# Scores in groups of three key chunks, and PSUM as three shared two-bank tiles: attention followed by an MLP mixer on one core

## The chip, the cores and the metric

The kernel runs on one core of one Trainium2 chip. The metric is the device time of one execution in microseconds (us), the median of several. The granted TensorE clock of one and the same kernel (its mean over the span, as a share of full speed) differs a little from run to run, mostly between 0.98 and 1.00, and so does the time.

Engine names in the profile: PE is TensorE's matmuls, PEld its weight loads, DVE is VectorE, ACT is ScalarE, POOL is GpSimd, SP the engine that issues most DMAs. Tile names: psS are scores, psO attention products, psR and psU the two token products (`tok1`, `tok2`), psG and psF the two channel products (`m_ch1`, `m_ch2`), pst and psT transposes. DVE evicts psO into x, psR into rt and psU into u; qk is the transposed q and k of a pair, pt the Exp of scores, gt the ReLU of psG, ost an output tile.

## The reference

Batch 8, 12 heads, 448 positions, head size 64; then a mixer MLP with 256 token units and 1536 channel units over the model width of 768.

```python
q_n = q / (norm(q) + 1e-6);  k_n = k / (norm(k) + 1e-6)
attn = softmax(q_n @ k_n.T / tau)
x    = concat_heads(attn @ v)                    # (8, 448, 768)
h    = relu(x.T @ w_tok1) @ w_tok2               # over positions
u    = x + h.T
out  = u + relu(u @ w_ch1) @ w_ch2               # over channels
```

## The kernel before

Work goes by pairs of heads, 48 of them (6 for each batch). The instructions of each engine are issued in the order in which the program writes them. For a pair there are four *score chunks* (112 keys by 448 queries, for two heads), each evicted by one Exp, then two *attention products* (`pv`, one for each head), two *token products* (`tok1`, `tok2`). The channel MLP of an earlier batch is cut into *units*, and units are fed in between, so that TensorE has something to do while other engines evict.

PSUM has eight banks. The Trainium skill, "PSUM — Partial Sum Buffer", section "Specifications (TRN2)", gives the same: 8 banks in a partition, 512 FP32 values each; the tiles of either kernel fill just eight. Before the change they are four single banks (`ps`, for everything but scores) and two two-bank tiles (`ps2`, for scores only).

```python
ps  = ctx.enter_context(tc.tile_pool(name="ps",  bufs=4, space=bass.MemoryType.PSUM))
ps2 = ctx.enter_context(tc.tile_pool(name="ps2", bufs=2, space=bass.MemoryType.PSUM))
# [cut]
def score(i, c):
    qk = pipe[i]["qk"][:].rearrange("p a c s -> p (a c s)")
    psS = ps2.tile([128, 2, 512], FP32, name=f"psS_{i}_{c}", tag="s")
    for hh in range(2):
        hb = hh * 64
        nc.tensor.matmul(psS[:, hh, 0:S], qk[hb:hb + 64, c * SC:c * SC + 128],
                         qk[hb:hb + 64, S:2 * S], start=True, stop=True)
    nc.scalar.activation(out=pts[i % 2][...], in_=psS[0:SC, :, 0:S], func=AF.Exp, scale=inv_tau)
# [cut: pv -> psO -> x by DVE; tok1 -> psR -> rt by DVE; tok2 -> psU -> u by DVE]
def m_ch1(b, ct):                                   # one unit: one bank
    psG = ps.tile([128, S], FP32, name=f"psG_{b}_{ct}", tag="b")
    for dt in range(DT):                            # 6 matmuls of 448 columns
        nc.tensor.matmul(psG[:], wc1t[...], ut[b][...], start=(dt == 0), stop=(dt == DT - 1))
    nc.scalar.activation(out=gt[...], in_=psG[:], func=AF.Relu)

def m_ch2(b, m, dh):                                # one unit: one bank
    psF = ps.tile([128, DH], FP32, name=f"psF_{b}_{m}_{dh}", tag="b")
    for ct in range(CT):                            # 12 matmuls of 384 columns
        nc.tensor.matmul(psF[:], gt[:, ct, lo:lo + 128], wc2t[...], start=(ct == 0), stop=(ct == CT - 1))
    # [cut: DVE adds u; for m == 3 in two adds of 64 partitions; after dh == 1 the DMAs out]
# [cut]
# main loop, pairs 7 to 48 (side work on q, k, v cut)
    score(i, 0); score(i, 1)
    feed(quota * 0.22)
    pv(i - 1, 0); pv(i - 1, 1)
    feed(quota * 0.28, least)
    score(i, 2); score(i, 3)
    feed(quota * 0.25, least)
    tok1(i - 1)
    feed(quota * 0.25, least)
    tok2(i - 1)
```

## Time and profile before

| | before |
|---|---|
| time, median of 3 first runs | 408.08 us (407.75 to 409.68) |
| span of the profiled run | 406.0 us, clock 0.982 |
| PE busy | 389.1 us, 96% |
| ACT, POOL, DVE busy | 59%, 54%, 51% |

These lines are from the page of the kernel before: the busy time of PE with its share of the span and its count of instructions, then the span in 40 slices, with the busy tenths of PE and the granted clock in tenths.

```profile
PE 389.1 (96%) x4146; PEld 240.4 (59%) x4146; DVE 206.4 (51%) x441; ACT 240.8 (59%) x392; POOL 218.5 (54%) x257
...
PE   6978799999999999999999999999999999999995
...
PEclk9868999999999999999999999999999999999999
```

PE is at 9 (90% or more) from slice 6 to the last but one. The clock is down only in the slices between 10 and 40 us; the trace has it halved from 9.1 to 12.5 and from 22.7 to 33.0 us.

The table by stretches of the same kernel: the stretch in us from the start, its length, then the busy time (and count) of PE, PEld, DVE, ACT and POOL, then the clock and the DMA share and rate.

```profile
62.00:100.00 38.00, 36.60 (x437) 22.84 (x435) 23.44 (x46) 27.54 (x55) 29.84 (x33) 1.00 0.98 208
100.00:140.00 40.00, 40.00 (x435) 23.79 (x432) 20.21 (x45) 27.44 (x44) 23.49 (x27) 1.00 0.79 165
...
300.00:340.00 40.00, 40.00 (x425) 24.18 (x425) 18.34 (x46) 22.11 (x33) 15.53 (x19) 1.00 0.47 102
```

In the stretches of 40 us shown PE is busy all the time. A busy PE is not by itself a PE at its peak, because the ends of matmuls are modelled. So the starts were read from the trace too. From one matmul to the next they are at the streaming rate: psG (448 columns) 189 ns, psF (384) 162, psR and psU (128) 56, psO (65) 29 to 33. Around scores they are not: the last matmul before a score takes 95 ns more than its rate, and the last score before another product takes 93 ns more.

The groups of instructions that matter, from the page: line, engine, operation, tiles, shapes, count, then busy us, mean ns of one, and after the second bar the idle time before them with its main releaser.

```profile
L321 PE MATMUL psG<-ut,wc1t 128*128 128x448 f16 x576 | 122.4, 353 | 0.0
L336 PE MATMUL psF<-wc2t,gt 128*128 128x384 f16 x672 | 116.6, 326 | 0.0
...
L340 DVE TENSOR_TENSOR ost<-psF,u 128x384 f32<-128x384 f32 (+1 forms) x64 | 35.7, 557 | 96.2 <-PE psF L336 96.0
L324 ACT ACTIVATE gt<-psG 128x448 f16<-128x448 f32 x96 | 52.3, 545 | 53.7 <-PE psG L321 53.5
...
L256 PE MATMUL psS<-qk 64*128 64x448 f16 x384 | 56.2, 363 | 3.5 <-ACT pt L258 2.7
```

PE has 3.5 us of idle time before scores in the whole span. Three lines of PE's timeline in the steady part (start, length, line, operation, count):

```profile
195.44 0.55 PE L256 MATMUL psS<-qk 64*128 64x448 f16 x4
195.92 1.19 PE L272 MATMUL psO<-vt,pt 112*128 112x65 f16 x32
196.95 1.30 PE L321 MATMUL psG<-ut,wc1t 128*128 128x448 f16 x6
```

A group of four score matmuls (two chunks) starts at 195.44 and the next product at 195.92. Two heads' matmuls run side by side in two halves of the array's rows, so two chunks take two streams of 0.19 us, which is 0.38; the group takes 0.48, and the product ahead of it is stretched by 0.1 as well.

**The ledger.** From the starts as the trace has them, the time from the first MLP matmul to the last matmul can be split. For each matmul the streaming time of its own columns (two side-by-side score matmuls count as one) is subtracted from the gap to the next start; each change between scores and other products is charged 0.0945 us; what is left of a gap counts as a wait where it is over 0.03 us, else as remainder. For the kernel before:

```
                streaming   changes         waits   remainder   first MLP matmul to last matmul
before          327.75      162 = 15.31      1.81     3.69        348.56 us
```

There is next to nothing to gain but the 15.31 us of changes (the text also calls them drains). That is what the change is after.

### The profile page before, as it was taken

How to read it: one execution, taken by the hardware profiler on the slowest of the kernel's cores; microseconds unless marked ns; L12 is line 12 of the kernel's file. 1: busy time of each engine (PE TensorE's matmuls, PEld its weight loads, DVE VectorE, ACT ScalarE, POOL GpSimd, SP SyncE). 2: the span in 40 equal slices, each digit the busy share in tenths (PEclk: the TensorE clock that was granted, in tenths of full speed). 3: DMA queues.
4: the chain of work that ended last, by engine and by line, in shares of the span. 5: the costliest groups of instructions: out<-in, count | busy, mean ns of one | idle time of the engine just before them, and what ended most of it. 6: DMA issues, size and time to landing. Idle time of an engine off the chain costs nothing.

```text
span 406.0 us, 10118 instructions
## 1 busy us (share of the span) xinstructions
PE 389.1 (96%) x4146; PEld 240.4 (59%) x4146; DVE 206.4 (51%) x441; ACT 240.8 (59%) x392; POOL 218.5 (54%) x257
## 2 busy tenths in 40 slices
PE   6978799999999999999999999999999999999995
PEld 5656566566555665656656655556655666655562
DVE  5767877655454466554555555635636345312031
ACT  5857789954676438773587437773588535521400
POOL 7797999948557480949175852949092800000000
PEclk9868999999999999999999999999999999999999
DMA  8999999978859786867759697978974433103022
GB/s 198 239 175 251 246 262 230 209 195 180 201 142 191 140 200 157 197 161 171 201 127 187 156 184 188 164 152 187 195 130 94 114 81 92 28 15 116 2 74 81
DMA packets 102590, 64.07 MB, mean 158 GB/s; under 512 B 61328, under 2 KB 98960, under 8 KB 102544
## 3 DMA queue, kind: packets, MB, share of 16 engines
q1 hardware_dynamic: 96928, 58.22, 64.0%
q0 software_dynamic: 5616, 5.21, 8.1%
q8 instruction: 32, 0.52, 0.6%
q14 instruction: 14, 0.11, 0.1%
HBM read 43.45 MB, written 11.01 MB: 134 GB/s over the span
## 4 chain that ended last, share of the span: by engine, by line
PE 87%; DMA 5%; DVE 4%; POOL 1%; issue 1%; ACT 1%; SPq 0%; DVEq 0%; POOLq 0%
PE psF L336 27%; PE psG L321 27%; PE psO L272 12%; PE psS L256 10%; PE psU L299 5%; PE psR L285 5%; DMA kf<-in_k_dram 4%; DVE ssq L198 2%; DMA qf<-in_q_dram 1%; DVE x L276 1%; PE pst L235 1%; POOL kq L221 0%; ACT sq L185 0%; DVE ost L340 0%; DVE rt L288 0%
## 5 line engine op out<-in xcount | busy, mean ns | idle before, releaser
L258 ACT ACTIVATE pt<-psS 112x896 f16<-112x896 f32 x192 | 166.2, 914 | 84.4 <-PE psS L256 84.1
L321 PE MATMUL psG<-ut,wc1t 128*128 128x448 f16 x576 | 122.4, 353 | 0.0
L336 PE MATMUL psF<-wc2t,gt 128*128 128x384 f16 x672 | 116.6, 326 | 0.0
L221 POOL TENSOR_TENSOR kq<-kf,rn 112x512 f16<-112x512 f32 x47 | 50.0, 1063 | 99.3 <-ACT rn L213 86.3
L336 PEld LDWEIGHTS <-gt 128*128 128x128 f16 x672 | 63.1, 98 | 43.4 <-issue 5.2
L340 DVE TENSOR_TENSOR ost<-psF,u 128x384 f32<-128x384 f32 (+1 forms) x64 | 35.7, 557 | 96.2 <-PE psF L336 96.0
L324 ACT ACTIVATE gt<-psG 128x448 f16<-128x448 f32 x96 | 52.3, 545 | 53.7 <-PE psG L321 53.5
L321 PEld LDWEIGHTS <-wc1t 128*128 128x128 f16 x576 | 51.3, 98 | 46.6 <-issue 8.2
L198 DVE TENSOR_REDUCE ssq<-sq 112x16 f32<-112x1024 f32 (+1 forms) x49 | 58.1, 1189 | 9.0 <-ACT sq L185 6.4
L272 PEld LDWEIGHTS <-pt 112*128 112x128 f16 x1536 | 53.5, 99 | 15.5 <-ACT gt L324 7.0
L256 PE MATMUL psS<-qk 64*128 64x448 f16 x384 | 56.2, 363 | 3.5 <-ACT pt L258 2.7
L272 PE MATMUL psO<-vt,pt 112*128 112x65 f16 x1536 | 59.3, 195 | 0.1
L302 DVE TENSOR_TENSOR u<-psU,x 128x512 f16<-128x512 f32 x48 | 33.1, 689 | 34.2 <-PE psU L299 34.2
L187 POOL TENSOR_TENSOR sq<-kf 112x512 f32<-112x512 f32 x46 | 47.7, 1037 | 3.9 <-DMA kf<-in_k_dram 3.4
L221 POOL TENSOR_TENSOR kq<-qf,rn 112x512 f16<-112x512 f32 x45 | 46.8, 1041 | 0.0
L288 DVE TENSOR_SCALAR rt<-psR 128x256 f16<-128x256 f32 x48 | 20.2, 421 | 46.8 <-PE psR L285 46.6
L276 DVE TENSOR_TENSOR x<-psO,rec 128x256 f16<-128x256 f32 x96 | 40.8, 425 | 3.3
L187 POOL TENSOR_TENSOR sq<-qf 112x512 f32<-112x512 f32 x39 | 40.5, 1037 | 0.0
L285 PE MATMUL psR<-x,w1t 128*128 128x128 f16 x384 | 29.8, 221 | 2.6 <-DVE x L276 2.6
L285 PEld LDWEIGHTS <-w1t 128*128 128x128 f16 x384 | 25.0, 99 | 11.6 <-issue 3.3
L299 PEld LDWEIGHTS <-w2t 128*128 128x128 f16 x384 | 25.9, 100 | 9.0 <-issue 2.1
L299 PE MATMUL psU<-rt,w2t 128*128 128x128 f16 x384 | 30.1, 223 | 0.4 <-DVE rt L288 0.2
(40 smaller groups left out, 156.0 us busy)
## 6 DMA issues: line engine op xcount, KB each, us to landing
qf<-in_q_dram SPq DMA_DIRECT2D x48, 224.0 KB, 3.8
kf<-in_k_dram SPq DMA_DIRECT2D x48, 224.0 KB, 3.7
vf<-in_v_dram SPq DMA_DIRECT2D x48, 224.0 KB, 3.7
out_dram<-ost SPq DMA_DIRECT2D x8, 336.0 KB, 3.1
wc1t<-in_moe_w_ch_dram POOLq DMA_DIRECT2D x4, 576.0 KB, 8.2
wc2t<-in_moe_w_ch_dram POOLq DMA_DIRECT2D x2, 1152.0 KB, 16.3
out_dram<-ost SPq DMA_DIRECT2D x8, 288.0 KB, 2.9
out_dram<-ost SPq DMA_DIRECT2D x8, 240.0 KB, 2.8
```

The costliest lines, as they stand in the source:

```text
L187: nc.gpsimd.tensor_mul(out=pipe[i]["sq"][:, a], in0=src, in1=src)
L198: nc.vector.tensor_reduce(out=half[i // HP]["ssq"][:, a0:a1, lo:lo + 2 * NCH], in_=pipe[i]["sq"][:, a0:a1], axis=AXX.X, op=ALU.add)
L221: (eng or nc.gpsimd).tensor_tensor(out=st["kqn"][:, a].rearrange("p c g e -> p g c e"), in0=side(i, a), in1=_bcast_free(rn, E), op=ALU.mult)
L256: nc.tensor.matmul(psS[:, hh, 0:S], qk[hb:hb + 64, c * SC:c * SC + 128], qk[hb:hb + 64, S:2 * S], start=True, stop=True)
L258: nc.scalar.activation(out=pts[i % 2][:, 2 * S * c:2 * S * (c + 1)].rearrange("p (h s) -> p h s", h=2), in_=psS[0:SC, :, 0:S], func=AF.Exp ...
L272: nc.tensor.matmul(psO[:, m, 0:E + 1], pts[i % 2][:, at:at + 128], vt[:, g, c, 0:E + 1], start=(c == 0), stop=(c == NCH - 1))
L276: nc.vector.tensor_tensor(out=st["x"][:, :, hh * E:(hh + 1) * E], in0=psO[:, :, 0:E], in1=_bcast_free(rec[:], E), op=ALU.mult)
L285: nc.tensor.matmul(psR[:, tt], w1t[:, w1[m], tt * 128:(tt + 1) * 128], st["x"][:, m], start=(m == 0), stop=(m == 3))
L299: nc.tensor.matmul(psU[:, m], w2t[:, tt, lo:lo + 128], st["rt"][:, tt], start=(tt == 0), stop=(tt == TT - 1))
L321: nc.tensor.matmul(psG[:], wc1t[:, dt, ct * 128:(ct + 1) * 128], ut[b][:, dt].rearrange("p m s -> p (m s)")[:, lo:lo + S], start=(dt == 0) ...
L324: nc.scalar.activation(out=gt[:, ct, (b % 2) * S:(b % 2 + 1) * S], in_=psG[:], func=AF.Relu)
L336: nc.tensor.matmul(psF[:], gt[:, ct, lo:lo + 128], wc2t[:, ct, dh * DH:(dh + 1) * DH], start=(ct == 0), stop=(ct == CT - 1))
```

## The change

Scores go in groups of three chunks, across the borders of pairs, so that there are fewer changes between scores and the rest. Three chunks need three two-bank tiles, which leaves two single banks. The MLP units are therefore made twice as large (two banks each) and share the three big tiles; a fixed pattern is replaced by a loop that goes by groups. The core of the diff, cut:

```diff
-    ps = ...tile_pool(name="ps", bufs=4, ...PSUM)
-    ps2 = ...tile_pool(name="ps2", bufs=2, ...PSUM)
+    ps = ...tile_pool(name="ps", bufs=2, ...PSUM)
+    ps2 = ...tile_pool(name="ps2", bufs=3, ...PSUM)
@@ [cut: three pt buffers; warm-up matmuls allot a tile each, 8 more of them in each of pairs 2 to 5, 10 fewer ahead of the loop] @@
     def m_ch1(b, ct):
-        psG = ps.tile([128, S], FP32, name=f"psG_{b}_{ct}", tag="b")
+        psG = ps2.tile([128, 2, 512], FP32, name=f"psG_{b}_{ct}", tag="s")
+        for j in range(2):
             [6 matmuls into bank j]
-        nc.scalar.activation(out=gt[:, ct, ...], in_=psG[:], func=AF.Relu)
+        nc.scalar.activation(out=gt[:, ct:ct + 2, ...], in_=psG[:, :, 0:S], func=AF.Relu)
@@ [cut: m_ch2 likewise, psF of two banks, one DVE add of 768 columns; m == 3: two adds of 64 partitions, for two batches] @@
+    def feed():                       # once a group, at least one unit
+        fed[0] += fed[1]
+        done = 0
+        while queue and (done == 0 or fed[0] > queue[0][0] / 2):
+            t, fn = queue.pop(0)
+            fn()
+            fed[0] -= t
+            done += 1
+
+    def refill(b):                    # at tok2 of a batch's last pair
+        while queue:
+            queue.pop(0)[1]()
+        queue.extend((ch2_units(b - 1) if b else []) + ch1_units(b))
+        fed[:] = [0.0, sum(t for t, _ in queue) / 8]
+        if b == B - 2:
+            queue.extend(ch2_units(b))
@@ main loop @@
+        chunks = [(i, c) for i in range(NPAIR + 1, NP_ALL) for c in range(NCH)]
+        groups = [chunks[j:j + 3] for j in range(0, len(chunks), 3)]
+        while u_next < NP_ALL:
+            [score() of the group; side work]
+            r_ok, u_ok = p_next, r_next
+            if seen.get(p_next, g) < g:          # all four chunks in earlier groups
+                pv(p_next, 0); pv(p_next, 1); p_next += 1; r_ok = p_next
+            elif r_next < p_next:
+                tok1(r_next); r_next += 1; u_ok = r_next
+            elif u_next < r_next:
+                tok2_of(u_next); u_next += 1
+            feed()
+            while u_next < u_ok: tok2_of(u_next); u_next += 1
+            while r_next < r_ok: tok1(r_next); r_next += 1
+            g += 1
```

## The prediction

> **What bounds the kernel now.** TensorE. The table by stretches shows PE busy 40.0 of 40 us in nearly every stretch from 100 to 340 us, at clock 1.00; ACT is busy 59%, DVE 51%. Idle PE lies before 62 us (about 10 us) and in the last 4 us. Starts of consecutive matmuls in the trace are at the streaming rate (psG 189 ns, psF 162, psO 32, psU and psR 56) except around scores: the last matmul before a score takes 95 ns more, the last score 93 ns more (282 instead of 189). The Trainium skill, "TensorEngine Tiling (Array Packing)", Key Properties, says that a change of tiling mode drains TensorE; scores are 64-row tiles, all else is not. The trace agrees: 0.189 us per score group, on the critical engine.
>
> **Removed.** Pairs 7 to 47 have 82 groups of two chunks now, 55 groups after: 27 x 0.189 = 5.1 us, all on the critical path. Fewer, wider evictions (a 448-wide ReLU takes 545 ns, an 896-wide Exp 914) save ACT and DVE: no gain.
>
> **Added, by mistake.** The refill for batch 6 puts batch 6's second channel product at the end of the queue; the refill for batch 7 empties the queue and puts the same product in again. Three units run twice: 72 matmuls of 162.5 ns = 11.7 us of PE, where PE has no idle time. The result stays right.
>
> **Added waits.** A group of three needs all three two-bank tiles, and the third is the one that the latest MLP unit filled. From that unit's last matmul start the trace has 0.38 us to the eviction; with 0.92 us for a wide ReLU (0.96 for a wide add, estimates) and 0.05 back, the tile is free 1.17 us after the unit's end. PE covers 0.475 us with two chunks and the drain, and 0.45 by each token product between. In program order the steady cycle is four groups for three pairs:
> - two groups end in both token products: no wait;
> - one ends in one: 0.24 us;
> - one has no attention product and nothing behind its unit: 0.69 us before the next third chunk, and 0.31 us before its own unit, which meets the first Exp still running.
> 1.24 us per cycle, 12 cycles: 15 us. Adds in two 64-partition halves (twice 0.96 us) and DVE lateness with two small PSUM banks instead of four: 5.5 us. Groups 6 to 8 find the queue empty and wait for Exp: 1.5 us. Together 22 us.
>
> **Start.** Three score tiles remove waits for Exp of 0.6 to 0.8 us, but two small banks tie PE to DVE, and warm-up matmuls are added (1.8 us, partly in idle time). Net 0, give or take 4. The half clock at 23 to 33 us may move.
>
> **Sum.** 408.1 - 5.1 + 11.7 + 22 = 436.7 us. Prediction 437, range 424 to 449. Faster by over 2%: 1%; within 2%: 4%; slower by over 2%: 95%.
>
> **What would show it.** 744 psF matmuls instead of 672; idle time before score matmuls rising from 3.5 us to over 10, released by ReLU (gt), output add (ost) or Exp (pt); PE busy near 92% instead of 96%, with dents between 60 and 340 us; the drain still near 93 ns per edge, but a third rarer; the end, after the last token product, about 12 us longer.
>
> **What would make it wrong.** If waits hide behind each other or wide evictions free their tile sooner, only the repeat less the drains remains (about 415). If two banks make PE wait for DVE at every attention product, it exceeds 450. If the queue repeats nothing, it is about 425.

## The result

| | before | after |
|---|---|---|
| time, median (lowest to highest), 4 runs each | 408.86 us (407.75 to 409.68) | 436.80 us (436.64 to 439.99) |
| ratio of the means, 95% interval | | 1.070 (1.065 to 1.076), slower |
| span of the profiled run, clock | 406.0 us, 0.982 | 434.9 us, 0.999 |
| PE busy | 389.1 us, 96% | 401.6 us, 92% |

A ratio is always the mean time of one kernel's fast runs over that of the other's of the same rounds, so it is not quite the ratio of the medians that are quoted.

The same lines of the page after the change:

```profile
PE 401.6 (92%) x4240; PEld 253.0 (58%) x4240; DVE 203.9 (47%) x412; ACT 234.8 (54%) x344; POOL 218.4 (50%) x258
...
PE   7787899789999998999999989999999989999995
...
PEclk9999999999999999999999999999999999999999
```

PE has dents now, an 8 in the busy tenths at almost regular distances, and 94 more instructions. By stretches:

```profile
62.00:100.00 38.00, 33.74 (x429) 21.77 (x428) 23.58 (x50) 29.12 (x53) 30.74 (x34) 1.00 0.92 194
...
140.00:180.00 40.00, 37.30 (x400) 23.36 (x397) 18.36 (x37) 19.53 (x26) 22.97 (x26) 1.00 0.74 178
...
300.00:340.00 40.00, 38.69 (x416) 24.00 (x415) 17.65 (x37) 25.09 (x35) 20.52 (x24) 1.00 0.46 104
...
380.00:420.00 40.00, 40.00 (x236) 22.95 (x235) 7.53 (x8) 5.50 (x6) 0.00 (x0) 1.00 0.20 60
```

Each stretch of 40 us between 100 and 380 us has lost one to three microseconds of PE; the one after 380 us is full. The groups:

```profile
L333 PE MATMUL psF<-wc2t,gt 128*128 128x384 f16 x744 | 124.7, 326 | 0.4 <-ACT pt L257 0.2
L321 PE MATMUL psG<-ut,wc1t 128*128 128x448 f16 x576 | 114.5, 352 | 0.2
...
L324 ACT ACTIVATE gt<-psG 128x896 f16<-128x896 f32 x48 | 44.0, 916 | 79.0 <-PE psG L321 78.5
L337 DVE TENSOR_TENSOR ost<-psF,u 128x768 f32<-128x768 f32 (+1 forms) x35 | 33.5, 957 | 113.1 <-PE psF L333 113.0
...
L255 PE MATMUL psS<-qk 64*128 64x448 f16 x384 | 55.0, 357 | 11.3 <-DVE ost L337 4.8
```

There are 744 psF matmuls where there were 672: 72 more, three units of 24. The idle time before scores is 11.3 us where it was 3.5, and its main releaser is the output add. The view of waits, PE's only (who waited for what, total us, how many times, longest):

```profile
PE psS L255 <- DVE ost L337: 4.8, 8, 0.7
PE psS L255 <- ACT gt L324: 4.2, 6, 1.6
PE pst L235 <- DVE rt L287: 3.7, 4, 1.1
PE psU L298 <- DVE rt L287: 3.0, 5, 0.7
```

And the timeline of the stretch after one of the units with half-partition adds:

```profile
161.48 1.94 DVE L337 TENSOR_TENSOR ost<-psF,u 64x768 f32<-64x768 f32 x2 [2.64 <-PE psF L333]
...
161.73 0.61 PE L284 MATMUL psR<-x,w1t 128*128 128x128 f16 x8
...
162.27 0.55 PE L255 MATMUL psS<-qk 64*128 64x448 f16 x4
...
163.48 0.36 PE L255 MATMUL psS<-qk 64*128 64x448 f16 x2 [0.66 <-DVE ost L337]
...
164.53 0.61 PE L298 MATMUL psU<-rt,w2t 128*128 128x128 f16 x8 [0.69 <-DVE rt L287]
...
164.97 2.43 PE L321 MATMUL psG<-ut,wc1t 128*128 128x448 f16 x12
...
167.44 0.92 ACT L324 ACTIVATE gt<-psG 128x896 f16<-128x896 f32 x1 [2.24 <-PE psG L321]
...
168.41 0.36 PE L255 MATMUL psS<-qk 64*128 64x448 f16 x2 [0.52 <-ACT gt L324]
```

Four score matmuls (two chunks) start at 162.27 and run at once. The third chunk starts at 163.48 and not at 162.65, because its tile is the one that the psF unit filled and DVE's two adds (from 161.48, 1.94 us) have not left it yet. `rt` comes behind them on DVE, and psU waits for it. After the psG unit of 164.97, with no product between it and the next group, the third chunk waits again, for the ReLU of 167.44 (0.92 us).

The idle time in these views is smaller than the wait. The view says 0.66 us before the chunk at 163.48, while its start is 0.82 us late. Matmuls' ends are modelled later than the next one could start: one of 448 columns is shown as 0.36 us and streams 0.19. The Trainium skill, "Perfetto Trace Analysis", section "Per-instruction lifecycle: what the profiler-reported window actually captures", says that TensorE's end time is estimated; this trace agrees. The ledger, which goes by starts, is used for sizes below:

```
                streaming   changes         waits   remainder   first MLP matmul to last matmul
before          327.75      162 = 15.31      1.81     3.69        348.56 us
after           339.26      108 = 10.21     25.21     3.23        377.90 us
difference      +11.51            -5.10    +23.40    -0.46        +29.34 us
```

Ahead of the first MLP matmul the changed kernel is 0.5 us earlier (50.0 against 50.5 us from the first warm-up matmul), so the spans differ by 28.9 us.

### The profile page after: what moved, and what is told of

The parts are those of the page before. It is cut to its first block, busy times and chain, and to the rows that moved or that the text cites. A ratio compares the mean times of both kernels' runs of the same rounds, so it can differ in the third digit from the quotient of the medians.

```text
span 434.9 us, 10171 instructions
## 1 busy us (share of the span) xinstructions
PE 401.6 (92%) x4240; PEld 253.0 (58%) x4240; DVE 203.9 (47%) x412; ACT 234.8 (54%) x344; POOL 218.4 (50%) x258
## 4 chain that ended last, share of the span: by engine, by line
PE 44%; POOL 20%; issue 19%; DVE 8%; DMA 5%; ACT 3%; SPq 0%; POOLq 0%; DVEq 0%
PE psF L333 18%; PE psG L321 14%; POOL sq L187 9%; POOL kq L221 8%; PE psO L271 6%; DMA kf<-in_k_dram 3%; DVE ost L337 3%; PE psS L255 3%; POOL vt L176 3%; PE psU L298 2%; DVE ssq L198 2%; DMA qk<-kq 1%; DVE u L301 1%; ACT gt L324 1%; PE pst L235 1%
## 5 line engine op out<-in xcount | busy, mean ns | idle before, releaser
L257 ACT ACTIVATE pt<-psS 112x896 f16<-112x896 f32 x192 | 163.1, 917 | 95.5 <-PE psS L255 95.3
L333 PE MATMUL psF<-wc2t,gt 128*128 128x384 f16 x744 | 124.7, 326 | 0.4 <-ACT pt L257 0.2
L321 PE MATMUL psG<-ut,wc1t 128*128 128x448 f16 x576 | 114.5, 352 | 0.2
L333 PEld LDWEIGHTS <-gt 128*128 128x128 f16 x744 | 71.7, 98 | 46.7 <-issue 1.1
L324 ACT ACTIVATE gt<-psG 128x896 f16<-128x896 f32 x48 | 44.0, 916 | 79.0 <-PE psG L321 78.5
L337 DVE TENSOR_TENSOR ost<-psF,u 128x768 f32<-128x768 f32 (+1 forms) x35 | 33.5, 957 | 113.1 <-PE psF L333 113.0
L321 PEld LDWEIGHTS <-wc1t 128*128 128x128 f16 x576 | 54.5, 98 | 47.4 <-issue 0.7
L255 PE MATMUL psS<-qk 64*128 64x448 f16 x384 | 55.0, 357 | 11.3 <-DVE ost L337 4.8
L271 PEld LDWEIGHTS <-pt 112*128 112x128 f16 x1536 | 52.2, 98 | 15.5 <-issue 6.2
L255 PEld LDWEIGHTS <-qk 64*128 64x128 f16 x384 | 15.9, 94 | 35.1 <-issue 18.1
L298 PEld LDWEIGHTS <-w2t 128*128 128x128 f16 x384 | 24.3, 98 | 13.8 <-issue 8.3
```

The lines of the kernel that those rows point to most:

```text
L257: nc.scalar.activation(out=pts[i % 3][:, 2 * S * c:2 * S * (c + 1)].rearrange("p (h s) -> p h s", h=2), in_=psS[0:SC, :, 0:S], func=AF.Exp ...
L271: nc.tensor.matmul(psO[:, m, 0:E + 1], pts[i % 3][:, at:at + 128], vt[:, g, c, 0:E + 1], start=(c == 0), stop=(c == NCH - 1))
L298: nc.tensor.matmul(psU[:, m], w2t[:, tt, lo:lo + 128], st["rt"][:, tt], start=(tt == 0), stop=(tt == TT - 1))
L321: nc.tensor.matmul(psG[:, j, 0:S], wc1t[:, dt, (ct + j) * 128:(ct + j + 1) * 128], ut[b][:, dt].rearrange("p m s -> p (m s)")[:, lo:lo + S ...
L324: nc.scalar.activation(out=gt[:, ct:ct + 2, (b % 2) * S:(b % 2 + 1) * S], in_=psG[:, :, 0:S], func=AF.Relu)
L333: nc.tensor.matmul(psF[:, dh, 0:DH], gt[:, ct, lo:lo + 128], wc2t[:, ct, dh * DH:(dh + 1) * DH], start=(ct == 0), stop=(ct == CT - 1))
```

## The experiments

The theory from the prediction has three parts: drains saved, a repeat of three units, and waits of the third chunk for the tile of the latest unit. The rival for the third part is that the two single banks, where there were four, tie PE to a late DVE.

### Without the repeat

```diff
-        queue.extend((ch2_units(b - 1) if b else []) + ch1_units(b))
+        queue.extend((ch2_units(b - 1) if 0 < b < B - 1 else []) + ch1_units(b))
```

> The changed kernel with one edit: the refill for the last batch no longer queues batch 6's second channel product a second time. Theory (the repeat is 72 matmuls of 162.5 ns on a TensorE without idle time there): 672 psF matmuls, and 11.7 us less than the changed kernel, about 425. Rival (the repeated units only fill time in which TensorE would have waited): less than 4 us gained, above 432.

Measured: 427.31 us (425.45 to 428.16), ratio to the kernel before 1.044 (1.039 to 1.049). PE's group of this run:

```profile
L333 PE MATMUL psF<-wc2t,gt 128*128 128x384 f16 x672 | 113.0, 326 | 0.6 <-ACT pt L257 0.4
```

The 72 matmuls are gone, and the ledger's streaming term falls from 339.26 to 327.56 us, that is 11.70. The medians differ by 9.5 us only (436.80 less 427.31). Most runs of this kernel had a lower clock, 0.985 to 0.991; its one run at 0.999 took 425.45 us, 11.2 less than the changed kernel's 436.64 at 0.999. In the profiled run (0.985) the clock is halved for 6.8 us behind a wait of 1.73 us at 79 us; the changed kernel has the same wait there, and its clock stays full. The first part of the gap to before is thus shown, and the rival (it only fills waits) fails.

### Units evicted in two halves

```diff
+        for j in range(2):
+            [6 matmuls into bank j]
+            nc.scalar.activation(out=gt[:, ct + j, ...], in_=psG[:, j, 0:S], func=AF.Relu)
-        nc.scalar.activation(out=gt[:, ct:ct + 2, ...], in_=psG[:, :, 0:S], func=AF.Relu)
```

(and the add of `m_ch2` in two halves in the same way; the repeat stays).

> The changed kernel with one edit: each two-bank MLP unit is evicted in two halves (ReLU 448 wide, add 384 wide), the first while the second half is being multiplied. The repeat stays. Theory (the third score chunk waits for the tile of the latest unit): the tile is free 0.79 us after the unit's end instead of 1.17, so the wait of 0.69 us falls to about 0.31 and the one of 0.24 to 0, and the long ones around the units with half-partition adds go: about 11 us less, 426, idle time before psS from 11.3 to about 5 us. Rival (two small PSUM banks tie TensorE to VectorE): within 2 us of the changed kernel, 435 to 439, and the waits before psS stay.

Measured: 504.19 us, ratio 1.234 (1.229 to 1.239), far from both. The waits of PE in this run:

```profile
PE psG L321 <- ACT gt L324: 43.7, 48, 2.8
PE psF L338 <- DVE ost L332: 22.4, 31, 1.2
```

All 48 psG units and all 31 psF units now have PE stand in their middle: the matmuls into the second bank came behind the eviction of the first. That this is because both belong to one tile is inferred, not tested here. The intended overlap did not come about in this program. What it does show is the third chunk. Its waits in the ledger (score to score) fall from 15.66 to 4.38 us, and the page's idle time before psS from 11.3 to 2.3 us, as the theory said, while the number of small banks is the same. In the steady part 11 waits are left, of 0.31 to 0.33 us each, where the changed kernel has 0.68 (psG) and 0.73 (psF), and those of 0.24 and 0.28 are gone: just what the expectation gave for an eviction half as wide.

### Groups of two

```diff
-        groups = [chunks[j:j + 3] for j in range(0, len(chunks), 3)]
+        groups = [chunks[j:j + 2] for j in range(0, len(chunks), 2)]
-        fed[:] = [0.0, sum(t for t, _ in queue) / 8]
+        fed[:] = [0.0, sum(t for t, _ in queue) / 12]
-        while queue and (done == 0 or fed[0] > queue[0][0] / 2):
+        while queue and fed[0] > queue[0][0] / 2:
```

> The changed kernel with scores in groups of two chunks (12 groups per batch instead of 8, units paced by their budget alone), PSUM as changed, the repeat kept. Theory (groups of three need all three tiles): the waits before the third chunk go, some 20 us, and 27 more groups drain for 5.1 us: about 421. Rival (the two small banks are the cost): waits stay, and the drains are added: 440 or more.

Measured: 473.74 us, ratio 1.159 (1.154 to 1.163). This run was badly made: groups with an attention product and no unit let `tok1` follow it at once, and the ledger has 28.5 us of waits from psO to psR, for DVE's x. The pacing was mended, and the run repeated:

```diff
+        while queue and (force and done == 0 or fed[0] > queue[0][0] / 2):   # force: group has an attention product
```

> The run in groups of two again, repeat kept, with the pacing mended: a group with an attention product always gets a unit behind it (in the first try it did not, and TensorE waited 28 us before psR for VectorE's x). Theory (groups of three need all three tiles): no waits before the third chunk, drains of 82 groups: about 421. Rival (the two small banks are the cost): 435 or more.

Measured: 435.54 us (435.26 to 436.08), ratio 1.065 (1.063 to 1.068). The total misses the expectation by 14 us and lies where the rival put it (435 or more), and yet the ledger does what the theory said of the third chunk: waits between scores fall from 15.66 to 0.57 us, the changes rise to 162 = 15.31 us. In their place stand 13.98 us between scores and psU and 3.88 us inside psO (these wait for Exp). The timeline shows the longest kind:

```profile
157.12 0.61 PE L284 MATMUL psR<-x,w1t 128*128 128x128 f16 x8
157.32 1.94 DVE L337 TENSOR_TENSOR ost<-psF,u 64x768 f32<-64x768 f32 x2 [2.66 <-DMA kf<-in_k_dram]
...
157.67 0.55 PE L255 MATMUL psS<-qk 64*128 64x448 f16 x4
...
159.30 0.42 DVE L287 TENSOR_SCALAR rt<-psR 128x256 f16<-128x256 f32 x1
159.78 0.61 PE L298 MATMUL psU<-rt,w2t 128*128 128x128 f16 x8 [1.56 <-DVE rt L287]
```

`tok1` at 157.12 is followed by only two chunks of scores before `tok2` of the same pair, and its `rt` sits on DVE behind the output adds. So the rival's sort of wait, a late DVE, does appear as soon as the order gives it room; it is a data wait for `rt`, not a wait for a free small bank.

### Products dealt out three to a group

Each group gets three of the twelve products that three pairs have: two ahead of the unit and one behind it. The repeat is taken out.

```diff
+            p = NPAIR + 1 + 3 * ((g - 2) // 4)
+            first, last = {2: ([(P0, p), (P1, p)], [(T2, p - 1)]),
+                           3: ([(T1, p), (P0, p + 1)], [(P1, p + 1)]),
+                           0: ([(T2, p), (T1, p + 1)], [(P0, p + 2)]),
+                           1: ([(P1, p + 2), (T2, p + 1)], [(T1, p + 2)])}[g % 4]
             [first]; feed(); [last]
```

> The changed kernel without the repeat (measured 427.3), and the attention and token products dealt out three to a group, one of them behind the unit; evictions wide as in the change. Theory: one product of 0.45 to 0.52 us behind each unit leaves about 0.25 us of the 0.69 us wait, in about 47 groups, so waits before psS stay near 12 us, but the waits of the group without an attention product (0.3 us before its unit, 0.8 us around half-partition adds) go: 417 to 421. Rival (waits come from the number of small banks): no change, 425 to 429.

Measured: 418.88 us (417.96 to 419.57), ratio 1.024 (1.021 to 1.027), within the theory's range. The waits before the third chunk are 0.24 us behind a psG unit with a token product, 0.17 with an attention product and 0.28 behind a psF unit, again and again (0.22 and 0.42 in places); the theory has 0.69 less 0.45, and 0.69 less 0.515. PE's timeline around one of them:

```profile
190.79 4.07 PE L333 MATMUL psF<-wc2t,gt 128*128 128x384 f16 x24
194.69 0.61 PE L298 MATMUL psU<-rt,w2t 128*128 128x128 f16 x8
195.23 1.03 PE L255 MATMUL psS<-qk 64*128 64x448 f16 x6
```

One product of 0.45 us stands between the unit and the scores; six score matmuls take 1.03 us to the end of the last where 0.74 is usual when they do not wait. In the steady part (after 93 us) the waits other than the third chunk's fall from 6.3 to 1.1 us, with the same two small banks. One part of the expectation failed: around the three units with half-partition adds the third chunk waits 0.98 to 1.05 us, where it was 0.82; only the 0.77 us before psU behind them went.

### The same with halves

```diff
   [mends of the three runs above together: no repeat, units evicted in halves, products three to a group]
```

> Groups of three with three mends: no repeat, units evicted in halves, and the attention and token products dealt out three to a group (two before the unit, one behind it), so that each group covers the first Exp (needs 0.77 us behind the scores) and the last unit's eviction (needs 0.31 us more than the 0.475 us that two chunks cover). Theory: no waits left in the steady part, the 5.1 us of drains saved in full: about 402 to 405, faster than the kernel before by about 1%. Rival (two small banks tie TensorE to VectorE): waits of 5 us or more before psO, psU or psR remain, 410 or above.

Measured: 482.71 us, ratio 1.181 (1.176 to 1.186). It was sent together with the halves above and has their fault: PE waits 43.8 us inside psG and 20.4 us inside psF. Its idle time before psS is 2.0 us. As a time it says nothing.

### ReLU by two engines at once

```diff
-        nc.scalar.activation(out=gt[:, ct:ct + 2, ...], in_=psG[:, :, 0:S], func=AF.Relu)
+        nc.scalar.activation(out=gt[:, ct, lo:lo + S], in_=psG[:, 0, 0:S], func=AF.Relu)
+        nc.vector.tensor_scalar_max(out=gt[:, ct + 1, lo:lo + S], in0=psG[:, 1, 0:S], scalar1=0.0)
```

(the repeat is out here too).

> The changed kernel without the repeat (427.3), and each first-product unit evicted after its last matmul by ACT (first bank) and DVE (second bank) at once, 0.55 us instead of 0.92. Theory: the third chunk's wait behind such a unit falls from 0.68 to about 0.3 and from 0.24 to 0, 6 times each: 3 to 5 us less, 422 to 424. Rival (VectorE is the late engine because of the two small banks): more work on VectorE makes it slower, 429 or more.

Measured: 439.53 us (439.24 to 440.27), ratio 1.075 (1.072 to 1.078). The time is where the rival put it. The timeline shows why:

```profile
171.91 2.43 PE L321 MATMUL psG<-ut,wc1t 128*128 128x448 f16 x12
...
174.38 0.55 ACT L325 ACTIVATE gt<-psG 128x448 f16<-128x448 f32 x1 [2.24 <-PE psG L321]
...
174.96 0.62 DVE L326 TENSOR_SCALAR gt<-psG 128x448 f16<-128x448 f32 x1 [1.82 <-ACT gt L325]
...
175.63 0.37 PE L255 MATMUL psS<-qk 64*128 64x448 f16 x2 [0.81 <-DVE gt L326]
```

The two evictions do not run at once: DVE's half starts at 174.96, when ACT's half (174.38, 0.55 us) has ended. The tile is occupied for 0.55 + 0.62 us and the step between them, some 1.21 us, instead of 0.92. The wait of the third chunk grows by just that: 0.97 us where it was 0.68, and 0.52 where it was 0.24 (ledger, five times each in the steady part), which is 0.28 to 0.29 more each. Besides, DVE's later `rt` costs 0.65 us before psU, eight times. So the run made the suspected cost 0.29 us longer where it should have made it 0.37 shorter, and the wait followed it to the hundredth.

> No repeat, products dealt out three to a group, first-product units evicted by ACT and DVE at once, second-product units evicted by DVE (first bank, with the add) and ACT (second bank, a copy, with the add later on POOL). Theory: the tile is free about 0.8 us behind the unit's end, and two chunks with the drain (0.475) and one product (0.45) cover 0.92: no waits in the steady part, 402 to 406, a little faster than the kernel before (408) by the 5 us of drains. Rival (two small banks): waits before psO, psU or psR of 5 us or more, above 410.

This run joined the two-engine evictions (of psF too, with an ACT copy and a later add on POOL) to the dealt-out products. Measured: 433.06 us (432.56 to 433.80), ratio 1.059 (1.056 to 1.062), a miss for the same reason: the evictions came one after another, and the ledger has 26.4 us between scores. Its trace also narrows down why: DVE's add out of the first bank starts (157.55 us) only when ACT's copy out of the second has ended (157.03, 0.49 us), while DVE and POOL then write their halves of the same ost tile at the same time (157.55 and 157.59). This points to the shared PSUM tile, and not to the shared output tile, as what puts one behind the other; no run separates the two.

### Half products on each side of the unit

The middle product of each group is cut in two, half ahead of the unit and half behind it.

```diff
+        for m, lo in enumerate(windows(b)):
+            if mid and m == 2:
+                mid()                    # feed()
```

The first try also had ACT copy the tile of the half-partition units out, and DVE add later:

```diff
+            nc.scalar.activation(out=o[...], in_=psF[:, :, 0:DH], func=AF.Copy)   # m == 3 only
             add(0, 64, b - 1, 3); add(64, 128, b, 0)                              # now out of SBUF
```

> The run that dealt the products out three to a group (418.9, with 50 waits of 0.17 to 0.28 us before the third chunk left), with the middle product of each group cut in two: half before the unit, half behind it; and the third-type unit with half-partition adds evicted by one ACT copy of 0.8 us, the adds then out of SBUF. Theory: each side of the unit is now covered to within 0.1 us (needs 0.77 before and 0.69 to 0.73 behind; has 0.68 to 0.78 and 0.68 to 0.77), so the waits before the third chunk fall from 14.9 to under 4 us, and the repeated 1 us ones go: 404 to 408, at or below the kernel before. Rival (the waits stem from something else that the order of products shifted by chance): waits before psS above 8 us, 412 or more.

Measured: 431.33 us (429.17 to 432.55), ratio 1.054 (1.049 to 1.059). The third chunk's waits in the steady part are gone, 0.14 us where the dealt-out run had 12.2. But the time is worse. The timeline at one of three such places:

```profile
261.46 2.96 DVE L343 TENSOR_TENSOR ost<-ost,u 64x768 f32<-64x768 f32 x2 [3.56 <-ACT ost L355]
...
261.85 1.76 POOL L221 TENSOR_TENSOR kq<-kf,rn 112x512 f16<-112x512 f32 x1
...
264.45 0.69 DVE L307 TENSOR_TENSOR u<-psU,x 128x512 f16<-128x512 f32 x1
...
265.20 1.50 PE L273 MATMUL psO<-vt,pt 112*128 112x65 f16 x24 [3.28 <-DVE u L307]
```

With both inputs in SBUF the two adds take 2.96 us together (1.24 and 1.69), where out of PSUM they took 0.96 each; POOL's operation meanwhile takes 1.76 us instead of 1.04. The same adds out of SBUF take 0.95 us each at 359 and 413 us, where POOL is idle, so it is POOL at work beside them that makes them longer. The Trainium skill, "SBUF — State Buffer", section "Who interferes with whom", says that a DVE instruction with two SBUF inputs contends with a GpSimd instruction that reads SBUF; the trace agrees, with these numbers. `u` comes behind the adds, psU's small bank stays occupied until then, and psO waits 3.28 us. The ledger has three such waits, of 3.35, 3.35 and 2.51 us. The third has no POOL beside it, so contention is only some 0.84 us of the first two; the rest is the order, in which two adds and `u` stand behind the ACT copy. Soon behind each wait comes a stretch of psG matmuls that start 0.37 us apart instead of 0.19: the clock had been halved (5.0 us in all). The Trainium skill, "TensorE: Matmul & The Clock Gate", section "Why this matters for your kernels", asks for no idle gaps of PE over about 3 us; the trace agrees for the two of 3.35 us, and 2.51 us was enough here too (shorter ones in other runs: last section).

Without the ACT copy:

> The run with the halved middle products again, without its ACT copy for the units with half-partition adds (that copy made VectorE add out of SBUF for 3 us while a small PSUM bank waited behind it, and TensorE stood 3.3 us three times). Theory: third-chunk waits of the steady part gone but for the three long ones of 1 us, some 4 us of small waits for VectorE's x and u in their place, the start of the steady part unchanged: 409 to 414, below the run with whole products (418.9). Rival (halving the products gains nothing by itself): 417 to 421.

Measured: 421.33 us (421.17 to 421.58), ratio 1.029 (1.027 to 1.032): a miss, no better than whole products, and just above the rival's range. The ledger splits it:

```
waits, us              up to 93 us   third chunk after 93   others after 93
after                  5.83          13.11                   6.27
products three each    4.51          12.20                   1.10
products halved        8.26           2.42                  10.03
```

(93 us is counted from the first warm-up matmul.) The third chunk's waits go as expected, but others of about the same size come: psR and psU wait for x, psO for a bank that u still holds, 0.04 to 0.35 us each, and 1.67 us of half-rate psF matmuls after a wait of 2.65 us for a transposed q and k at 90 us.

> The same, and the six units of batch 0 spread over the first nine groups instead of the first six, so that no three groups in a row have no unit. Theory: the waits of 70 to 95 us after the start (about 4 to 7 us: no unit to cover the Exps, qk late) shrink by half: 2 to 4 us less than the run beside it, 407 to 411, level with the kernel before. Rival (these waits come from POOL and VectorE, busy near 90% there): no change.

```diff
-        fed[:] = [0.0, sum(t for t, _ in queue) / 8]
+        fed[:] = [0.0, sum(t for t, _ in queue) / (8 if b else 9)]     # and no forced unit before group 9
```

Measured: 420.45 us (419.48 to 420.63), ratio 1.026 (1.024 to 1.029): a miss. The wait for q and k fell from 2.65 to 1.13 us, and new waits at 55 to 68 us took most of it back.

### More changes between scores and the rest

In the kernel before, the groups of two chunks are pulled apart where a unit can go between.

```diff
-                score(i, 0)
-                score(i, 1)
+                score(i, 0)
                 [side work]
                 feed(quota * 0.22)
+                score(i, 1)
@@
-                score(i, 2)
-                score(i, 3)
-            feed(quota * 0.25, least)
+                score(i, 2)
+            feed(quota * 0.25, least)
+                score(i, 3)
             tok1(i - 1)
```

> The kernel before with its score groups of two chunks pulled apart where a unit can go between (the same work, 236 changes between scores and other products after the first MLP matmul instead of 162). Theory (each change drains TensorE for 0.0945 us): 74 x 0.0945 = 7.0 us more than the kernel before, ratio 1.014 to 1.020. Rival (the extra time at a change only hides something that would be waited for anyway, so that the change's 5.1 us were never to be had): ratio within 0.995 to 1.007.

Measured: 416.73 us (416.40 to 418.40), ratio 1.019 (1.014 to 1.023). The total fits, but the ledger says that it fits partly by chance: 236 changes at 0.0945 us are 22.30 us, 7.0 more than before, with the remainder only 0.8 us larger, so the price of one change is the same within 0.01 us (many of the changes back cost 103 ns here where they cost 93); there are also 6.4 us of new waits (scores for Exp, psO for v's cast), and the first MLP matmul is 5.5 us earlier than in the profile of the kernel before, whose clock was halved for a while between 9 and 33 us and this one's was not. The earlier start and the new waits, all before 80 us, nearly cancel. The price of a change stands; the size of this run's loss is no separate proof of it.

## Why the prediction was right

The time was predicted as 437 us (424 to 449) and measured as 436.8.

| term | predicted | measured (ledger) |
|---|---|---|
| fewer changes between scores and the rest | -5.1 | -5.10 (54 fewer, counted, at 0.0945) |
| three units repeated | +11.7 | +11.5 (run without: 11.7 in streaming, 9.5 in medians, 11.2 at equal clock) |
| waits, together | +22 | +23.4 |
| of these: third chunk and first Exp in the steady cycle | 15 | 12.7 |
| of these: half-partition adds, late DVE | 5.5 | 5.7 |
| of these: groups 6 to 8 and the rest of the early part | 1.5 | 4.3 |
| of these: end of the loop | not foreseen | 0.7 |
| start | 0 | -0.5 |
| remainder | not foreseen | -0.5 |

That the sum came so close is luck: the steady cycle was put 2.3 us too high, the early part 2.8 too low, and the base of 408.1 us, a median of three runs, became 408.86 with the fourth. What was earned is the terms and the range.

- **The bound and the drains.** Right. The changes fell from 162 to 108, and the extra time of each edge is the same in both kernels within 0.01 us (after: 96 ns from psR to psS, 93 to 104 from psS to psO). The saving is real, and four times as much is lost elsewhere.
- **The repeat.** Right, and read from the program alone: nothing in the profile of before could have told it. 744 psF matmuls appear, the result stays right, and the end after the last token product is 11.7 us longer (57.05 against 45.35), as forecast.
- **The third chunk's wait.** Right, and the runs make it a cause and not only an account. Behind a unit with no product the wait is 0.68 us for psG and 0.73 for psF (predicted 0.69), with one token product 0.24 and 0.28 (predicted 0.24). A product behind each unit takes off its own length; an eviction 0.29 us longer adds 0.28 to 0.29 us; one half as wide leaves 0.31 to 0.33; groups of two, which need no third tile, bring it from 15.66 to 0.57 us. The number of small banks was the same in all of these.
- **The wait for the first Exp.** Sized a little too large: 0.20 us and 0.06 ahead of it, against 0.31.
- **Half-partition adds and DVE.** Right in size: three places with 0.82 us before the third chunk and 0.77 us before psU, 4.8 us together, and six times 0.15 us before psO, whose small bank DVE's u has not left yet: in the steady part these 0.9 us are all that the trace shows of waits for a small bank.
- **Early groups.** Too small, 1.5 against 4.3 us. The prediction counted waits for Exp in three groups without units. The ledger has, among others, 1.73 us before a score at 78 us and 0.94 us from psO to psR, where no unit covers DVE's x. The first is not the groups' alone: the run with more changes, in the order of before, has 1.85 us at the same place (77 us), and in both the eviction stands behind ACT's work on the norms.
- **The start.** Right as a sum, but in part by luck, for the sum hides two parts that were not separated. The view of waits of after has 3.7 us of pst waiting for DVE's rt (four times), which before has not, and which is what two small banks do there; against it stands that the profiled run of before had its clock halved for a while and this one had not. The run with more changes helps: up to pair 7 its program is that of before, its clock was not halved, and it reaches the first score of pair 7 at 42.4 us, counted from the first warm-up matmul, where before has 48.4 and the changed kernel 47.4. So at equal clock the changed kernel starts 5.0 us later. The 5.9 us that the half clock had cost before are gone again by pair 11 (72.5 against 72.6 us). What a later start is worth at the end of the changed kernel stays open.

The prediction's alternative, "If two banks make PE wait for DVE at every attention product, it exceeds 450", did not happen. But the runs with halved products and with groups of two show that a late DVE is next in line: once the third chunk's wait is covered, 8 to 16 us of waits for x, u and rt stand in its place. Whether more small banks or only another order of products would remove those was not tried. No version here beats the kernel before; the best, at 418.9 us, has its 5 us of drains saved and 17.8 us of waits.

## What to carry to other kernels

When a bottleneck engine is already full, count what a regrouping needs at once: three chunks that need all three tiles turn the eviction of the latest unit into a wait of PE, 0.7 us in one group of four, and this outweighs 0.19 us saved for each group avoided. Size such a wait as eviction latency less the work that stands between, both read from the trace, group by group in the order of issue; here that came within a few hundredths. And read a rewritten queue for what it does at its last refill: a repeat gives a right result and shows only in a count of instructions.

## What the Trainium skill lacked or had wrong

- "TensorEngine Tiling (Array Packing)", "Key Properties", says that a change of tiling mode drains TensorE but gives no size. Here one change from 128- or 112-row to 64-row products costs 93 to 96 ns and one back 93 to 104 ns, with 108, 162 and 236 changes in a kernel.
- "TensorE: Matmul & The Clock Gate", "Why this matters for your kernels", puts the harmful gap at over about 3 us. Shorter waits were followed by half-rate matmuls here: 2.65 us (psF 0.32 us apart instead of 0.16, for about 3.4 us), 2.51 us, 1.73 us in the run without the repeat, and 1.83 us eleven times in the first try of groups of two. Others were not: 2.63 us in the first run with halves, 1.73 us in the changed kernel, 1.83 us three times. The page says (Part 1) that the window in which activity is counted is free-running; whether that decides between the two outcomes is not shown here.
- "SBUF — State Buffer", "Who interferes with whom", gives no time for a DVE add with two SBUF inputs beside GpSimd. Here two such adds of 64x768 took 1.24 and 1.69 us beside POOL and 0.95 without it, and POOL's multiplication 1.76 instead of 1.04.
- No page has the whole time from a PSUM tile's last matmul until the tile is free for the next. Here it was 0.38 us from the last matmul's start to the eviction, the eviction (0.92 us for a 128x896 ReLU, 0.96 for a 128x768 add), and some 0.05 us back.
- No page warns that evicting a two-bank tile in parts may not overlap: in these programs a second engine's half (0.62 us) came after the first's (0.55 us), and matmuls into one bank after the eviction of the other (43.7 us in 48 units).
